# A mixture-of-experts kernel on one core: the routing's arithmetic, the filler matmuls and the order of routing, conversion and weight splits around the first expert are rewritten

## The chip, the cores and the metric

The kernel runs on one core of one Trainium2 chip. The metric is device time in microseconds (us), the median of three runs. The five engines are named as in the profile: PE (TensorE; its weight loads are PEld), DVE (VectorE), ACT (ScalarE), POOL (GpSimd) and SP (SyncE, which here only issues DMAs). Every engine works through its own instructions in program order; an instruction that has to wait holds up all that stand behind it on that engine.

## The reference, cut to what matters

```python
# 1. retention attention: B=4, H=8, S=768, D=64 -> x of 3072 x 512
state = gamma * state + k_t v_t^T;  y_t = 0.125 * q_t state
# 2. routing: 3072 tokens, 8 experts, at most cap = 384 tokens each
for idx in argsort(-(x @ w_gate).flatten()):
    tok, e = idx // 8, idx % 8
    if assigned[tok] < 0 and counts[e] < cap:
        assigned[tok] = e; counts[e] += 1
out[assigned == e] = relu(x[assigned == e] @ w1[e]) @ w2[e]
# 3. dense layer on all tokens, d_ff = 2048
h = out @ w_in
return (max(h, 0) + log1p(exp(-abs(h)))) @ w_out
```

## The kernel before

**Stages.** `Attn` computes the attention in 24 blocks of 128 tokens, stores each block of x to memory (`xd`) and keeps the logits on chip. Beside it `Conv` turns `w_in` from 64-bit to 32-bit floats. Then `Route.phase(0)` finds the first expert that fills up, and the list of its 384 tokens; `fetch_x` (L692) gathers their rows from `xd` with three indirect DMAs that POOL issues. `Ffn.emit` (L835) then works through the eight experts: 24 products of the expert layer (`m1`, `m2`), 16 of the dense layer's first half (`f1`) and 16 of its second (`f2`), always for the 384 tokens of one expert. Every matmul operand is split in a high and a low part, so that each product takes three matmuls: ACT copies the high part, DVE subtracts it to get the low one.

**Routing.** A phase takes each open token's best expert and its logit as a 32-bit key, and looks for the highest key at which some expert has 384 takers. It does so in three levels (bits from 21 up, 10 to 20, 0 to 9), each with a coarse and a fine pass. A pass compares all keys with 46 (or 32) thresholds (DVE, `G`, L429), counts by expert (24 matmuls, L436), compares with the places left (`ind`, L487), counts the thresholds that hold (one matmul, L490) and reduces (`ksat`, L493). The fine pass's threshold comes from `ksat` (`thr`, L476); at its end `base` (L498) is formed, and the next level's keys (`lo`, `kf`, `kx`, L463 to L467). After the levels come the expert (`inc` to `es`, L503 to L528), the mask `mem` (L531 to L534), prefix sums over tokens (two matmul steps), the position of each token as one-hot rows (`ohq`, L567), and the list `ix` (L586). Then the bookkeeping for the next phase (L590 to L615). Phase 0 has nothing beside it: its steps follow each other directly, and in between PE gets filler matmuls (`hum`, L892, 128x512, results unused). The later phases are generators: `emit` calls `route()` once or every other time per product, and `route()` runs to the next `yield`. Their matmuls write a tile `rt`.

**Late conversion.** `w_out` is converted during phase 0 and the first expert: 32 halves of 256 columns. A piece is: `size` (ACT `cA` L270, POOL `cA` L271, ACT `cB` L272), then in one step DVE `cB` (L285), in the next DVE `cA` (L287) and the POOL sum (L288, writes `wol`). There are two `cB` buffers. The kernel before calls `size` for the next piece after this piece's sum. Phase 0 takes two steps in each of the four passes of levels 1 and 2; in the first expert one or two steps are taken after each product, before `route()`. `weights` (L859) splits the weights (`split_w`, L654) up to four products ahead; for a piece of `w_out` it first forces the conversion so far (`until`).

**Order.** Everything is issued in the order in which the Python code runs (a manual schedule); no planner moves instructions.

## Time and profile before

| | us |
|---|---|
| median of three runs | 1018.38 |
| lowest and highest run | 1016.86, 1020.95 |
| the profiled execution | 1018.63 |
| its span in the profile | 1016.9 |
| PE busy | 994.5 (98% of the span) |
| DVE busy | 637.5 (63%) |
| ACT busy | 579.9 (57%) |
| POOL busy | 160.2 (16%) |

Attention lasts until about 112 us of the span, phase 0 and the first gather until 148.5, the first expert until about 257, the other seven experts about 108 us each. PE busy includes fillers, so the busy share says little in phase 0; there the chain of work that ended last (each instruction with what released it) is the view to read. A bracket at the end of a timeline row gives the idle time of the engine before it and what ended it.

### The profile page before, as it was taken

The numbers are of one execution on the slowest core, as the hardware profiler recorded it, in microseconds if no ns is written. First come the engines' busy times: TensorE is split into PE (matmuls) and PEld (weight loads), VectorE is DVE, ScalarE is ACT, GpSimd is POOL, SyncE is SP. The second block draws the span as 40 slices with busy tenths as digits, with TensorE's granted clock in tenths as the row PEclk, the third lists the DMA queues.
The fourth block names the chain that finished last, engine by engine and source line by source line (L and its number), as shares of the span: only waits on it lengthen the run. The fifth ranks groups of instructions, "written<-read, shape, count | busy, mean of one in ns | idle before, by whom it ended". The sixth has DMA issues, their size and how long they took to land.

```text
span 1016.9 us, 19118 instructions
## 1 busy us (share of the span) xinstructions
PE 994.5 (98%) x7319; PEld 899.3 (88%) x7319; DVE 637.5 (63%) x1620; ACT 579.9 (57%) x1250; POOL 160.2 (16%) x185
## 2 busy tenths in 40 slices
PE   9999889999999999999999999999999999999997
PEld 8888669887998889998998899899989999999996
DVE  6989678879666656755575566555665644444442
ACT  5999425777446653665456635654366536653663
POOL 1655223556101010100110010001010010000001
PEclk9999789999999999999999999999999999999999
DMA  9998234224412023200410031103210250013000
GB/s 367 414 415 357 95 115 159 87 71 121 119 39 63 2 68 100 61 1 25 143 57 7 22 125 53 32 11 105 63 32 4 80 166 1 1 57 111 1 1 31
DMA packets 40603, 96.05 MB, mean 94 GB/s; under 512 B 5312, under 2 KB 5568, under 8 KB 40512
## 3 DMA queue, kind: packets, MB, share of 16 engines
q1 hardware_dynamic: 36528, 82.16, 23.9%
q0 software_dynamic: 3840, 12.59, 3.7%
q8 instruction: 57, 0.93, 0.4%
q14 instruction: 34, 0.28, 0.1%
q10 hardware_dynamic: 144, 0.09, 0.0%
HBM read 82.23 MB, written 12.58 MB: 93 GB/s over the span
## 4 chain that ended last, share of the span: by engine, by line
PE 75%; issue 12%; POOL 4%; DVE 4%; ACT 3%; DMA 1%; another core or an unknown queue 0%; POOLq 0%; ACTq 0%
PE h L684 11%; PE h L687 11%; PE h L685 10%; PE acc L782 7%; PE acc L783 7%; PE acc L787 7%; PE acc L676 3%; PE acc L678 3%; PE acc L677 3%; PE pA L130 2%; PE pY L158 2%; PE pX L183 2%; PE rt L436 2%; POOL wol L288 1%; POOL cA L271 1%
## 5 line engine op out<-in xcount | busy, mean ns | idle before, releaser
L748 DVE SCALAR_TENSOR_TENSOR gf<-h,sp 128x384 f32<-128x384 f32 x128 | 71.2, 556 | 186.7 <-ACT sp L746 186.7
L684 PE MATMUL h<-x2h,wih 128*128 128x384 f32 x512 | 175.6, 343 | 1.5 <-DVE xl L672 1.5
L685 PE MATMUL h<-x2h,wil 128*128 128x384 f32 x512 | 172.5, 337 | 0.0
L782 PE MATMUL acc<-whi,gh 128*128 128x512 f32 x384 | 153.3, 399 | 0.0
L783 PE MATMUL acc<-wlo,gh 128*128 128x512 f32 x384 | 151.3, 394 | 0.0
L744 ACT ACTIVATE sp<-h 128x384 f32<-128x384 f32 x128 | 62.4, 487 | 135.6 <-PE h L687 125.3
L668 ACT ACTIVATE h1h<-h 128x384 fp32r<-128x384 f32 x64 | 31.4, 491 | 147.2 <-PE h L687 105.1
L687 PE MATMUL h<-x2l,wih 128*128 128x384 f32 x512 | 112.2, 339 | 0.9 <-DVE x2l L672 0.8
L787 PE MATMUL acc<-whi,gl 128*128 128x512 f32 x384 | 111.2, 396 | 0.8 <-DVE gl L762 0.8
L795 POOL DMA_INDIRECT out_dram<-rows,ix x24 | 24.2, 1007 | 500.0 <-ACT rows L793 496.6
L684 PEld LDWEIGHTS h<-x2h,wih 128*128 128x128 f32 x512 | 96.2, 188 | 5.2 <-DVE xl L672 1.8
L685 PEld LDWEIGHTS h<-x2h,wil 128*128 128x128 f32 x512 | 96.2, 188 | 3.4
L687 PEld LDWEIGHTS h<-x2l,wih 128*128 128x128 f32 x512 | 91.3, 188 | 3.1 <-DVE x2l L672 3.1
L662 DVE TENSOR_TENSOR wlo<-wraw,whi 128x512 fp32r<-128x512 f32 x128 | 86.6, 691 | 6.5 <-ACT whi L661 6.4
L662 DVE TENSOR_TENSOR wlo<-wol,whi 128x512 fp32r<-128x512 f32 x128 | 88.9, 698 | 0.9 <-ACT whi L661 0.9
L684 PE MATMUL h<-xh,whi 128*128 128x384 f32 x256 | 88.2, 345 | 0.7 <-ACT xh L671 0.7
L787 PEld LDWEIGHTS acc<-whi,gl 128*128 128x128 f32 x384 | 72.0, 188 | 18.6 <-DVE gl L762 1.4
L676 PE MATMUL acc<-h1h,whi 128*128 128x384 f32 x256 | 88.4, 345 | 0.0
L661 ACT ACTIVATE whi<-wraw 128x512 fp32r<-128x512 f32 x128 | 76.6, 624 | 17.3 <-DMA wraw<-in_moe_w_dram 16.0
L678 PE MATMUL acc<-h1l,whi 128*128 128x384 f32 x256 | 86.1, 336 | 0.0
L685 PE MATMUL h<-xh,wlo 128*128 128x384 f32 x256 | 86.1, 336 | 0.0
L677 PE MATMUL acc<-h1h,wlo 128*128 128x384 f32 x256 | 86.1, 336 | 0.0
(199 smaller groups left out, 1902.7 us busy)
## 6 DMA issues: line engine op xcount, KB each, us to landing
wraw<-in_moe_w_dram SPq DMA_DIRECT2D x128, 256.0 KB, 2.6
qk_t<-in_qk_dram SPq DMA_DIRECT2D x24, 512.0 KB, 8.6
kv_t<-in_kv_dram SPq DMA_DIRECT2D x24, 512.0 KB, 9.0
raw<-in_moe_w_in_dram SPq DMA_DIRECT2D x16, 512.0 KB, 8.7
raw<-in_moe_w_out_dram SPq DMA_DIRECT2D x32, 256.0 KB, 3.0
xd<-xs SPq DMA_DIRECT2D x24, 256.0 KB, 4.9
rows<-xd,ix POOLq DMA_INDIRECT x24
out_dram<-rows,ix POOLq DMA_INDIRECT x24
```

The source lines that it names most:

```text
L661: nc.scalar.activation(hi, raw, AF.Copy)
L662: nc.vector.tensor_tensor(lo, raw, hi.bitcast(FT), op=OP.subtract)
L676: nc.tensor.matmul(ps, wh, ah, start=start, stop=False)
L677: nc.tensor.matmul(ps, wl, ah, start=False, stop=False)
L678: nc.tensor.matmul(ps, wh, al, start=False, stop=stop)
L684: mm(ps, wh(d), ah[:, d], start=d == 0, stop=False)
L685: mm(ps, wl(d), ah[:, d], start=False, stop=False)
L687: mm(ps, wh(d), al[:, d], start=False, stop=d == 3)
L748: nc.vector.scalar_tensor_tensor(g, ps, 0.0, a, op0=OP.max, op1=OP.add)
L782: nc.tensor.matmul(ps, gh[:, s], wh, start=f == 0, stop=False)
L783: nc.tensor.matmul(ps, gh[:, s], wl, start=False, stop=False)
L787: nc.tensor.matmul(ps, gl[:, s], wh, start=False, stop=f == 15)
```

## The change

1. **Routing arithmetic.** `kx` and the thresholds are scaled by 1/256. The coarse thresholds become constants (`coarse`), numbered so that no pass has to build them. A new `prepare` forms the next level's keys without the base (`kp`) beside the pass before, so that after `base` one operation gives `kx`; `kf` follows after the compare. The matmul after a fine pass multiplies by 4096 (`upto[46, 4096]`). The expert `inc` is read from the last pass's counts (`is_equal` with `k`) instead of a further mask, sum and matmul (which only the last phase keeps). The list's position is masked with 127 in integers.
2. **Filler.** `hum` is 128x256 instead of 128x512; 8, 5, 6, 9, 2, 16 and 30 of them where there were 6, 3, 6, 6, 1, 9 and 16; six more behind the bookkeeping's matmul, and six between the row transposes of the first expert. Phase 0 takes four conversion steps, one each in the first level's fine pass, the second's coarse one and both of the third, instead of eight.
3. **First rows.** `weights(3)` (three splits, and the loads they set free) moves behind the whole of phase 0; the third row tile of the first expert is copied in two halves.
4. **Conversion.** `size` of the next piece moves ahead of this piece's sum, into the step before.
5. **First expert.** `route()` comes before the conversion steps; conversion begins one product earlier; pieces of `w_out` are split two products ahead instead of four; the next expert's rows are fetched behind the first `f1` that finds the list made, not at `f1` number 10. Phase 2 does not begin before the second expert's row transposes, and in the other experts routing pauses during the last two `m2`.

The diff, cut to its core:

```diff
@@ Conv.run
             v.scalar_tensor_tensor(B, w1, UPPER, B, op0=OP.bitwise_and, op1=OP.bitwise_or)
+            if p + self.lead < N:
+                ready.append(self.size(p + self.lead))
             yield
             v.tensor_scalar(A, A, 3, 0x3fffffff, op0=OP.logical_shift_left, op1=OP.bitwise_and)
             nc.gpsimd.tensor_tensor(F, A, B, op=OP.add)
-            if p + self.lead < N:
-                ready.append(self.size(p + self.lead))
             yield
@@ Route
+    def prepare(self, s, sh, mask, off):
+
+        v = self.nc.vector
+        v.tensor_scalar(self.lo[:, s], self.ik[:, s], sh, mask, op0=OP.logical_shift_right, op1=OP.bitwise_and)
+        v.tensor_scalar(self.kp[:, s], self.kf[:, s], -1.0, 4096.0, op0=OP.max, op1=OP.mult)
+        v.scalar_tensor_tensor(self.kp[:, s], self.lo[:, s], off, self.kp[:, s], op0=OP.add, op1=OP.add)
+
@@ Route.phase
             if l:
-                lo = T([128, N], I32, "lo")
-                v.tensor_scalar(lo, self.ik, sh, span - 1, op0=OP.logical_shift_right, op1=OP.bitwise_and)
-                v.tensor_scalar(self.kf, self.kf, base, 4096.0, op0=OP.subtract, op1=OP.mult)
-                off = -4096.0 if l == 1 else 0.0
-                v.scalar_tensor_tensor(self.kf, lo, off, self.kf, op0=OP.add, op1=OP.add)
-                v.tensor_scalar(self.kx, self.bc(self.kf, N, 2), -1.0, 5000.0, op0=OP.max, op1=OP.min)
+                v.tensor_scalar(self.kx, self.bc(self.kp, N, 2), base, S, op0=OP.subtract, op1=OP.mult)
...
-                    fill(l)
+                    if l and not fine:
+                        v.tensor_scalar(self.kf, self.kp, base, 3000.0 if l == 1 else 1.0, op0=OP.subtract,
+                                        op1=OP.min if l == 1 else OP.add)
+                    if l == 1 and fine:
+                        self.prepare(all, 0, 1023, 4096.0)
+                    if i and not l and not fine:
+                        self.prepare(all, 10, 2047, 0.0)
+                    fill(2 * l + fine)
...
-                hum(6 if st == 1 else 3)
+                hum(9 if l == 2 and fine else 6 if fine else 5)
...
+        else:
+            v.tensor_tensor(inc, ps[:, 64:64 + E], k.to_broadcast([128, E]), op=OP.is_equal)
...
-        hum(1)
+        hum(2)
...
-        hum(9)
+        hum(16)
...
-        hum(16)
+        hum(30)
...
+        hum(6)
@@ Ffn.xt
+        if i == 0 and g == T3 - 1:
+            for d in (slice(0, 2), slice(2, 4)):
+                nc.scalar.activation(self.xh[:, d, s], ps[:, d], AF.Copy)
+            nc.vector.tensor_tensor(self.xl[:, :, s], ps, self.xh[:, :, s].bitcast(FT), op=OP.subtract)
+            return
@@ Ffn.emit
         for g in range(T3):
+            if g:
+                self.hum(ps, 6)
             self.xt(0, g)
...
                 while self.listed <= i + 1:
                     self.route()
+                if i + 1 not in self.xg:
+                    self.fetch_x(i + 1)
+            self.weights(at[n] + 4, at[n] + 2)
+            fn(i, f)
+            if fn == self.f1 and f > 1 and self.listed > i + 1 and i + 1 not in self.xg:
                 self.fetch_x(i + 1)
-            self.weights(at[n] + 4)
-            fn(i, f)
-            if i == 0 and n > 3:
+            step += 1
+            hold = self.phase == 1 and self.gen is None if i == 0 else fn == self.m2 and f > 5
+            if not hold and (self.listed <= i + 1 or step % 2 == 0):
+                self.route()
+            if i == 0 and n > 2:
                 for _ in range(1 + n % 2):
                     self.late.step()
-            step += 1
-            if self.listed <= i + 1 or step % 2 == 0:
-                self.route()
...
+    def hum(self, ps, n):
+        a = self.win[0][:, 0]
+        for _ in range(n):
+            self.nc.tensor.matmul(ps[:, 0:256], a[:, 0:128], a[:, 0:256], start=True, stop=True)
@@ Ffn.start
-            for _ in range(2 if level else 0):
+            for _ in range(level in (1, 2, 4, 5)):
                 self.late.step()
...
-            elif mark == "list":
-                self.fetch_x(0)
-                self.weights(3)
+        self.weights(3)
```

DVE in phase 0, from the first level's fine pass to the second level's first compare (before first, then the change; `ind` closes a pass, `cB` is a conversion step):

```order
L476 SCALAR_TENSOR_TENSOR thr<-ksat,jio 128x46
L429 TENSOR_TENSOR G<-kx,thr 128x552
L429 TENSOR_TENSOR G<-kx,thr 128x368
L429 TENSOR_TENSOR G<-kx,thr 128x184
L487 TENSOR_TENSOR ind<-pS,rem 128x8
L493 TENSOR_REDUCE ksat<-pS 128x1
L498 SCALAR_TENSOR_TENSOR base<-ksat 128x1
L463 TENSOR_SCALAR lo<-ik 128x24
L464 TENSOR_SCALAR kf<-kf,base 128x24
L466 SCALAR_TENSOR_TENSOR kf<-lo,kf 128x24
L467 TENSOR_SCALAR kx<-kf 128x48
L474 TENSOR_SCALAR thr<-jio 128x46
```

and in the changed kernel:

```order
L485 SCALAR_TENSOR_TENSOR thr<-ksat,jio 128x46
L435 TENSOR_TENSOR G<-kx,thr 128x552
L435 TENSOR_TENSOR G<-kx,thr 128x368
L435 TENSOR_TENSOR G<-kx,thr 128x184
L285 SCALAR_TENSOR_TENSOR cB<-raw,cB 128x256
L503 TENSOR_TENSOR ind<-pS,rem 128x8
L510 TENSOR_REDUCE ksat<-pS 128x1
L513 SCALAR_TENSOR_TENSOR base<-ksat 128x1
L478 TENSOR_SCALAR kx<-kp,base 128x48
L435 TENSOR_TENSOR G<-kx,coarse_81 128x552
```

Four operations between `base` and the next compare are gone, and a conversion step (`cB`) now stands ahead of `ind`.

DVE in the first expert, at the matmuls of phase 1's third level (`gf`, `gl` belong to the dense layer's first half; `ind` is what PE's `rt` matmul waits for):

```order
L762 TENSOR_TENSOR gl<-gf,gh 128x384
L748 SCALAR_TENSOR_TENSOR gf<-h,sp 128x384
L287 TENSOR_SCALAR cA<-cA 128x256
L285 SCALAR_TENSOR_TENSOR cB<-raw,cB 128x256
L487 TENSOR_TENSOR ind<-rt,rem 128x8
```

and in the changed kernel:

```order
L783 TENSOR_TENSOR gl<-gf,gh 128x384
L769 SCALAR_TENSOR_TENSOR gf<-h,sp 128x384
L503 TENSOR_TENSOR ind<-rt,rem 128x8
L289 TENSOR_SCALAR cA<-cA 128x256
L285 SCALAR_TENSOR_TENSOR cB<-raw,cB 128x256
```

The two conversion operations moved behind `ind`.

## Rows read from the trace of the kernel before

**Rows 1.** Busy PE, PEld, DVE, ACT, POOL by stretch; granted clock, DMA share, GB/s.

```profile
112.10:148.50 36.40, 31.04 (x256) 22.11 (x255) 26.77 (x116) 8.34 (x18) 10.39 (x12) 0.77 0.38 119
187.00:250.00 63.00, 58.52 (x362) 51.24 (x362) 52.88 (x144) 45.81 (x105) 38.55 (x41) 1.00 0.33 98
250.00:1005.00 755.00, 753.65 (x4730) 691.70 (x4729) 433.84 (x1083) 410.88 (x799) 42.26 (x62) 1.00 0.17 52
```

**Rows 2.** Chain that ended last, phase 0 to first product: start, us, what.

```profile
117.25 2.77 PE pA L894 x6
...
143.05 4.09 DMA rows<-xd,ix
...
148.53 0.44 PE h L684
```

**Rows 3.** Timeline of DVE in phase 0: start, us, engine, line, operation.

```profile
116.87 0.17 DVE L487 TENSOR_TENSOR ind<-pS,rem 128x8 bf16<-128x8 f32 x1 [0.47 <-PE pS L436]
...
117.49 0.16 DVE L498 SCALAR_TENSOR_TENSOR base<-ksat 128x1 f32<-128x1 f32 x1
...
118.59 0.87 DVE L429 TENSOR_TENSOR G<-kx,thr 128x552 bf16<-128x552 f16 x3
119.38 0.41 DVE L285 SCALAR_TENSOR_TENSOR cB<-raw,cB 128x256 int32<-128x256 int32 x1
...
120.70 0.17 DVE L487 TENSOR_TENSOR ind<-pS,rem 128x8 bf16<-128x8 f32 x1 [0.71 <-PE pS L436]
...
123.26 0.17 DVE L487 TENSOR_TENSOR ind<-pS,rem 128x8 bf16<-128x8 f32 x1 [0.28 <-PE pS L436]
...
124.20 0.43 DVE L464 TENSOR_SCALAR kf<-kf,base 128x24 f32<-128x24 f32 x1
...
127.08 0.17 DVE L487 TENSOR_TENSOR ind<-pS,rem 128x8 bf16<-128x8 f32 x1 [0.65 <-PE pS L436]
...
129.14 0.17 DVE L487 TENSOR_TENSOR ind<-pS,rem 128x8 bf16<-128x8 f32 x1
...
131.94 0.17 DVE L520 TENSOR_TENSOR inc<-pS,rem 128x8 f32<-128x8 f32 x1 [0.45 <-PE pS L517]
...
139.57 0.16 DVE L586 SCALAR_TENSOR_TENSOR ix<-pS,ix 128x3 int32<-128x3 f32 x1
```

**Rows 4.** Timeline of PE in phase 0: the matmul on `mem`, the fillers after the list.

```profile
133.95 0.18 PE L537 MATMUL pS<-ones,mem 128*128 128x1 bf16 x1
...
139.20 5.49 PE L894 MATMUL pA<-wih 128*128 128x512 f32 x16
```

**Rows 5.** One microsecond of phase 0, columns as in rows 1.

```profile
119.00:120.00 1.00, 1.00 (x8) 0.48 (x7) 1.00 (x5) 0.00 (x0) 0.00 (x0) 0.50 0.00 0
```

**Rows 6.** Timeline of ACT: the first late piece's second copy.

```profile
116.92 0.42 ACT L272 ACTIVATE cB<-raw 128x256 int32<-128x256 uint32 x1
```

**Rows 7.** Timeline of POOL in phase 0: a conversion operation beside the routing.

```profile
123.75 0.84 POOL L271 TENSOR_SCALAR cA<-cA 128x256 f32<-128x256 f32 x1
```

**Rows 8.** Timeline of POOL: last issue of a later gather, beside no other transfer.

```profile
327.00 0.95 POOL L697 DMA_INDIRECT rows<-xd,ix  x1 [0.30 <-issue]
```

**Rows 9.** The stretch behind that gather's landing, columns as in rows 1.

```profile
330.50:331.50 1.00, 1.00 (x6) 0.81 (x5) 1.00 (x3) 0.97 (x3) 0.00 (x0) 1.00 0.00 0
```

**Rows 10.** Who waited for whom, 148 to 256 us: total, times, longest.

```profile
ACT cB L272 <- POOL wol L288: 10.9, 10, 3.0
...
DVE cA L287 <- POOL cA L271: 7.4, 8, 1.4
...
PE h L684 <- DVE xl L672: 1.5, 1, 1.5
PE rt L490 <- DVE ind L487: 1.4, 1, 1.4
...
PE acc L787 <- DVE gl L762: 0.8, 1, 0.8
PE rt L543 <- DVE tb L540: 0.8, 1, 0.8
```

More of the change, by code (lines that the diff above doesn't have):

```diff
@@ L442, in first_part @@
         yield
-        self.compare(c0, c1, self.t0, 46)
+        self.compare(c0, c1, self.coarse[46], 46)
         yield
         self.nc.vector.tensor_scalar(self.kf[:, c0:c1], self.sg[:, c0:c1], 1025.0, None, op0=OP.add)
+        yield
+        self.prepare(slice(c0, c1), 10, 2047, 0.0)
     def phase(self, i, slow=True, hum=lambda n: None, fill=lambda l: None):
@@ L489, in phase @@
                     yield
-                nc.tensor.matmul(ps[:, 64:64 + E], self.upto[J], ind, start=True, stop=True)
-                hum(6 if st == 1 else 3)
+                f = 4096.0 if fine and l < 2 else 1.0
+                nc.tensor.matmul(ps[:, 64:64 + E], self.upto[J, f], ind, start=True, stop=True)
+                hum(9 if l == 2 and fine else 6 if fine else 5)
                 k = T([128, 1], FT, "ksat", bufs=2)
                 v.tensor_reduce(k, ps[:, 64:64 + E], axis=AX.X, op=OP.max)
-                if top is None:
-                    top = k
-                else:
+                if fine:
@@ L497, in phase @@
                     base = T([128, 1], FT, "base")
-                    v.scalar_tensor_tensor(base, top, float(s1), k, op0=OP.mult, op1=OP.add)
-        if base is None:
+                    v.scalar_tensor_tensor(base, top, J * f, k, op0=OP.mult, op1=OP.add)
+                top = k
+        inc = T([128, E], FT, "inc")
+        if last:
             base = 0.0
-        g2 = T([128, 2, N], BF, "g2")
-        gx = T([128, N, 2], BF, "gx")
-        v.tensor_scalar(gx, self.bc(self.kf, N, 2), base, None, op0=OP.is_ge)
@@ L512, in phase @@
-        v.tensor_scalar(g2[:, 1], self.kf, base, None, op0=OP.is_gt)
-        for _ in gap(2):
-            yield
-        if ps is None:
-            ps = self.psum_tile()
-        nc.tensor.matmul(ps[:, 128:128 + E], self.ones, rs[:, 0], start=True, stop=True)
-        hum(6)
-        inc = T([128, E], FT, "inc")
-        v.tensor_tensor(inc, ps[:, 128:128 + E], self.r, op=OP.is_ge)
+            gx = T([128, N, 2], BF, "gx")
+            v.tensor_scalar(gx, self.bc(self.kf, N, 2), base, None, op0=OP.is_ge)
@@ new lines, in phase @@
+            gg = T([128, N, E], BF, "gg")
+            v.tensor_tensor(gg.rearrange("p n (a m) -> p n a m", m=2),
+                            self.oe.rearrange("p n (a m) -> p n a m", m=2),
+                            gx[:, :, None, :].to_broadcast([128, N, E // 2, 2]), op=OP.mult)
+            rs = T([128, E], BF, "rs")
+            with nc.allow_low_precision("counts up to 24"):
+                v.tensor_reduce(rs, gg.rearrange("p c e -> p e c"), axis=AX.X, op=OP.add)
+            for _ in gap(2):
+                yield
@@ L521, in phase @@
+            ps = self.psum_tile()
+            nc.tensor.matmul(ps[:, 64:64 + E], self.ones, rs, start=True, stop=True)
+            v.tensor_tensor(inc, ps[:, 64:64 + E], self.r, op=OP.is_ge)
+        else:
+            v.tensor_tensor(inc, ps[:, 64:64 + E], k.to_broadcast([128, E]), op=OP.is_equal)
+        g2 = T([128, 2, N], BF, "g2")
+        v.tensor_scalar(g2[:, 0], self.kf, base, None, op0=OP.is_ge)
         pr = T([128, E], FT, "pr")
         v.tensor_tensor(pr, inc, self.desc, op=OP.mult)
+        v.tensor_scalar(g2[:, 1], self.kf, base, None, op0=OP.is_gt)
@@ L611, in phase @@
             yield
-        nc.tensor.matmul(ps[:, 136:136 + E], self.ones, rs[:, 1], start=True, stop=True)
+        nc.tensor.matmul(ps[:, 136:136 + E], self.ones, rn, start=True, stop=True)
+        hum(6)
         d2 = T([128, E], FT, "d2")
@@ L841, in emit @@
             n += g[3] is not None
+        ps = self.rps.tile([128, 512], FT, name="rt")
         for g in range(T3):
+            if g:
+                self.hum(ps, 6)
             self.xt(0, g)
@@ L885, in route @@
         self.gen = None
+    def hum(self, ps, n):
+        a = self.win[0][:, 0]
+        for _ in range(n):
+            self.nc.tensor.matmul(ps[:, 0:256], a[:, 0:128], a[:, 0:256], start=True, stop=True)
     def start(self, ps):
-        a = self.win[0][:, 0]
-        def hum(n):
-            for _ in range(n):
-                self.nc.tensor.matmul(ps, a[:, 0:128], a[:, 0:512], start=True, stop=True)
+        hum = lambda n: self.hum(ps, n)
         self.keys = [g[3] for g in self.plan(self.R.E) if g[3]]
```

89 lines of the change are left out of this document (45 added, 44 removed).

## The prediction

> **What bounds the kernel now.** I read the busy time by stretch first. From 250 to 1005 us PE is busy in 753.65 of 755 us [rows 1]: there nothing is to be had, and the change takes no matmul out of it. Two stretches are left. Phase 0 with the first gather, 112.1 to 148.5, takes 36.4 us in which PE does no product of the experts. In 187 to 250 PE stands still for 63.00 - 58.52 = 4.48 us, and by the waits that is four single waits, on `xl` 1.5, `ind` 1.4, `gl` 0.8 and `tb` 0.8, all DVE's [rows 1, 10]. So the change can win at most 4.5 us in the first expert, and in phase 0 what it takes from a chain. That chain is the view to read there: it runs through DVE operations and, which the busy share hides, through the fillers, as the 2.77 us of six fillers at 117.25 [rows 2]. The reader is to see that a filler that is still running when the compare is ready holds up the count behind it on PE.
>
> **Phase 0, part by part.** Times are from the start of `ind` in one pass to the start of `ind` in the next [rows 3].
>
> *A conversion step ahead of the first count.* The first fill now stands in the first level's fine pass, so DVE meets `cB` before the `ind` that ran at 116.87. That `cB` needs ACT's copy of the first piece of `w_out`, which ended at 116.92 + 0.42 = 117.34 since the load had just landed [rows 6]; with its own 0.41 [rows 3], `ind` comes at 117.75. Queued behind the waiting `cB` are `ind`, `ksat` and everything of the next pass. Loss 0.9.
>
> *Coarse passes of levels 2 and 3.* They took 120.70 - 116.87 = 3.83 and 127.08 - 123.26 = 3.82. From `base` to the compare there were six links in 118.59 - 117.49 = 1.10, some 0.2 each; two are left, 0.4. The clock is granted at 0.50 (the level of 1.2 GHz) at 119 [rows 5], and a filler of 512 columns takes 2.77 / 6 = 0.46, so one of 256 columns 0.23 at that level. In the changed pass the six fillers end 0.4 + 1.4 = 1.8 us after `ind`, the first half of the compare 0.6 + 0.4 + 0.5 = 1.5 after it; the 24 counts need about 0.75 (in the fine pass that ended at 129.14 they fit into 2.06 with everything else). Sum 2.5 to 2.6 in place of 3.8: gain 1.3 each, 2.6 together.
>
> *Fine passes.* 123.26 - 120.70 = 2.56 and 129.14 - 127.08 = 2.06. Five half fillers end 0.4 + 1.15 = 1.55 after `ind`, plus 0.75: 2.3 each. Gain 0.26, loss 0.24: nothing.
>
> *From the last pass to the mask.* From `ind` 129.14 to `inc` 131.94 are 2.80 us: `ksat`, `base`, a mask, a product, a sum and a matmul behind fillers. Now `inc` follows `base` (0.62 after `ind`, as 116.87 to 117.49) at 0.8, with one more small operation on the path: gain 1.8. The matmul on `mem` then began at 133.95 [rows 4], seven links of 0.2 behind `inc` being 133.4: the fillers held it 0.5. Nine half fillers at the low level (2.1) end before the mask does: gain 0.5. Together 2.3.
>
> *To the list.* From 133.95 to `ix` at 139.57 are 5.62. One operation goes from the positions, two move behind the first `ohq`, two are swapped for two: gain 0.3. The sixteen half fillers, 3.7 us at the low level, end as the last `ohq` arrives.
>
> Together -0.9 + 2.6 + 0 + 2.3 + 0.3 = 4.3 us at `ix`. The three new operations of `prepare` behind the last compare add under 0.1 here; in the attention they lie beside its matmuls (nine of 0.2 us, 1.8 if that cover failed). The `kp` operations that move into the passes lie beside the counts.
>
> *The rule on the shared port.* A DVE operation of the routing that meets a POOL operation of the conversion is stretched: `kf` at 124.20 took 0.43 beside `cA` at 123.75, where a link is 0.2 [rows 3, 7]. The Trainium skill, SBUF — State Buffer, "Who interferes with whom", speaks against putting `size` one step earlier: DVE in a two-port mode and GpSimd exclude each other, and the later one blocks for the whole instruction. By it each meeting could cost the 0.84 of that POOL operation; the row shows 0.2. There are now two to four such meetings in phase 0 as before, so the sum stays.
>
> **Gather and first product.** From `ix` to the first product are 148.53 - 139.57 = 8.96. The last gather was issued at 143.05 and took 4.09 to land [rows 2] beside three weight loads, which `weights(3)` now sets free only after the gather. Alone, a last issue at 327.00 had landed by 330.50 [rows 8, 9], 3.5: gain 0.6, and 0.3 from copying the last tile in two halves. Against it stand 30 + 6 + 6 + 6 fillers on PE ahead of the last transposes. Sixteen whole ones took 5.49 [rows 4] at a mixed clock; thirty half ones are fifteen whole: 5.2. With three times six half ones at the full clock (half of 0.23 each, 0.7 per six), three sets of transposes of 0.45, and 0.7 to the product, that is 0.2 before `ix` + 5.2 + 2.1 + 1.4 + 0.7 = 9.2. So PE and not the gather would be last: I take +0.2 of gain, with bounds of +0.9 (full clock throughout, gather last) and -2 (most fillers at the low level). Phase 0 gives 4.3 + 0.2 = 4.5, bounds 2.3 and 5.6. DVE's three `wlo`, moved behind the bookkeeping (3 us), end about 6 us after `ix`, before the products want them.
>
> **The first expert.** DVE's lateness behind the four waits has causes that the change takes on. It waited 7.4 us in eight places for POOL's `cA` [rows 10], since that stood behind the piece before's sum in POOL's queue; now it stands ahead. `ind` loses the two conversion operations in front of it (0.5 of its 1.4), and four links of the pass. The rows are fetched one `f1` earlier, off the time of the transposes whose `xl` cost 1.5. A phase loses about 1.7 us of DVE work, two splits move later; two pieces come in from phase 0 (1.4 us). I take 2.5 of 4.5, bounds 0 and 4.4.
>
> What is added is a wait on ACT. With two `cB` buffers, the copy for a piece needs the sum two pieces back, and it is now asked one step after that sum instead of two. Queued behind it are `gh`, `sp` and the weight copies, for which PE waits. ACT waited 10.9 us there in ten places already, 3.0 at most [rows 10].
>
> **Sum.** 4.5 + 2.5 = 7.0. The profiled execution took 1018.63, the median is 1018.38: 1018.38 - 7.0 = 1011.4.
>
> **Rivals.**
> - *The first expert gives nothing:* the ACT wait takes the place of DVE's. For it: 10.9 us already; against it: `gh` is wanted two products after it is made. 1018.4 - 4.5 = 1013.9.
> - *Fillers at the low clock:* thirty run before the chip grants the full clock, transposes come late. For it: 0.77 mean clock in the stretch [rows 1]. Gain 2.3 + 2.5: 1013.6.
> - *The chain is not shortened:* the first `cB` waits longer than the row says, since the load lands when it lands, and counts at the low clock fill what the links give back. Each coarse pass then gives 0.7 instead of 1.3 and the loss is 2: phase 0 gives 2.2, the first expert 0 to 1: 1015.7.
> - *Slower:* ACT becomes the bound of 187 to 250. It is busy 45.81 of 63 [rows 1], 17.2 free. Thirty pieces over some 100 us are 19 here; at the mean wait of today, 1.1, one for each piece costs 21, and from 0.9 per piece on PE waits. To end slower it must eat 4.5 more, from 1.15 per piece; at 1.5, 28.5 - 17.2 - 4.5 = 6.8 lost: 1025.
>
> **How the numbers follow.** Chances: forecast 0.50 (1008.3 to 1013.2), first expert nothing 0.18, low clock 0.13, chain not shortened 0.13, slower 0.06. The range of 1008.0 to 1016.0 takes the first four and the bounds 5.6 + 4.4 and 2.3 + 0. A measurement here can tell 0.5% from no change, which is 5.1 us, 1013.3. Faster: nearly all of the forecast (0.48) and four tenths of the next two (0.12), 0.60; slower 0.05; same 0.35.
>
> **What would show it.** `ind` of the first fine pass about 0.9 us late with `cB` ahead of it; coarse passes of 2.5; `ix` near 135.2; the first product near 144; idle PE in the first expert under 2.5 us, and DVE's wait for POOL's `cA` nearly gone. ACT's wait for the sum well above 10.9 us would show the rival, and transposes that follow a filler without a gap, at a granted clock of 0.50, the other. Wrong would be a shift anywhere behind 250 us.

## The result, and the profile after

The changed kernel takes 1030.62 us (median of five runs, 1029.97 to 1031.05), the kernel before 1019.28 beside it (1016.86 to 1020.95). The ratio is 1.0112, with a 95% interval of 1.0095 to 1.0129: it is **slower by about 11 us**, where 7 us of gain were forecast and 1008 to 1016 was the range. The profiled execution has a span of 1029.3 us against 1016.9.

The first thing to do is to cut the span at marks that both kernels have: the first mask product of the attention, the last row of `L` (the attention's end), and the first product of the experts. Of the kernel before, from DVE's timeline (start, us, engine, line, operation, and in brackets what it waited for):

```profile
7.09 1.29 DVE L134 TENSOR_TENSOR at<-pA,ctab 128x512 f32<-128x512 f32 x2 [3.46 <-PE pA L130]
...
112.13 0.19 DVE L186 TENSOR_REDUCE L<-pX 128x8 f32<-128x32 f32 x1 [1.26 <-PE pX L183]
```

and of the changed kernel, with the marks of phase 0 that answer to [rows 3], and from PE's timeline the first product:

```profile
6.57 1.29 DVE L134 TENSOR_TENSOR at<-pA,ctab 128x512 f32<-128x512 f32 x2 [2.74 <-PE pA L130]
...
114.59 0.19 DVE L186 TENSOR_REDUCE L<-pX 128x8 f32<-128x32 f32 x1 [1.26 <-PE pX L183]
...
120.06 0.16 DVE L503 TENSOR_TENSOR ind<-pS,rem 128x8 bf16<-128x8 f32 x1
122.61 0.17 DVE L503 TENSOR_TENSOR ind<-pS,rem 128x8 bf16<-128x8 f32 x1 [0.21 <-PE pS L442]
125.06 0.17 DVE L503 TENSOR_TENSOR ind<-pS,rem 128x8 bf16<-128x8 f32 x1
127.62 0.17 DVE L503 TENSOR_TENSOR ind<-pS,rem 128x8 bf16<-128x8 f32 x1 [0.29 <-PE pS L442]
129.96 0.17 DVE L503 TENSOR_TENSOR ind<-pS,rem 128x8 bf16<-128x8 f32 x1 [0.59 <-PE pS L442]
130.66 0.16 DVE L533 TENSOR_TENSOR inc<-pS,ksat 128x8 f32<-128x8 f32 x1
...
137.87 0.16 DVE L600 SCALAR_TENSOR_TENSOR ix<-pS,ix 128x3 int32<-128x3 f32 x1
...
146.11 0.45 PE L700 MATMUL h<-xh,whi 128*128 128x384 f32 x1 [0.47 <-ACT xh L728]
```

With the first product of before at 148.53 [rows 2] this gives three stretches:

| stretch | before | after | difference |
|---|---|---|---|
| attention: first mask product to last row of `L` | 105.04 | 108.02 | +2.98 |
| phase 0: last row of `L` to first product | 36.40 | 31.52 | -4.88 |
| first product to the end of the span | 868.37 | 883.19 | +14.82 |

(The other 0.52 are the start: the first mask product came 0.52 us sooner.) Phase 0 did what was forecast. The loss lies in the other two, above all behind the first product. By stretch, with the columns of [rows 1]:

```profile
187.00:250.00 63.00, 55.00 (x324) 47.68 (x323) 44.41 (x120) 38.14 (x89) 31.34 (x36) 0.95 0.27 80
250.00:1005.00 755.00, 749.42 (x4695) 689.47 (x4694) 431.01 (x1067) 413.00 (x804) 47.73 (x69) 1.00 0.18 54
```

In 187 to 250 PE is idle for 8.00 us where it was idle for 4.48, but DVE and ACT work less as well: DVE 44.41 in place of 52.88, ACT 38.14 in place of 45.81. No engine has become the bound; all of them wait, and for each other. Behind 250 the lateness goes on for a while: 5.58 us idle in place of 1.35. For whom they wait, 148 to 256 us, answering to [rows 10] (total, times, longest; `whi` and `wlo` are the high and the low part of a piece of weights):

```profile
POOL wol L290 <- DVE cA L289: 35.2, 17, 4.4
ACT cB L272 <- POOL wol L290: 33.0, 19, 3.9
...
DVE wlo L678 <- ACT whi L677: 16.5, 15, 1.6
...
PE rt L507 <- DVE ind L503: 2.9, 3, 1.7
...
PE rt L559 <- DVE tb L556: 2.9, 1, 2.9
...
PE h L700 <- DVE xl L688: 2.2, 1, 2.2
...
PE acc L804 <- DVE wlo L678: 1.5, 1, 1.5
```

ACT's wait for POOL's sum went from 10.9 us to 33.0, and DVE's wait for ACT, `wlo` for `whi`, from 1.1 us to 16.5. The row of the kernel before is

```profile
DVE wlo L662 <- ACT whi L661: 1.1, 2, 0.7
```

DVE's wait for POOL's `cA` (7.4) is gone, as the prediction said, and what came in its place is dearer. One turn of it, from the timelines of DVE, ACT, POOL and PE:

```profile
213.36 0.45 DVE L285 SCALAR_TENSOR_TENSOR cB<-raw,cB 128x256 int32<-128x256 int32 x1
213.78 0.16 DVE L564 COPY tot<-rt 128x1 f32<-128x1 f32 x1
...
216.04 0.31 DVE L587 TENSOR_TENSOR rh<-dd,cidb 128x144 bf16<-128x144 f32 x1
216.27 0.29 DVE L289 TENSOR_SCALAR cA<-cA 128x256 int32<-128x256 int32 x1
...
216.64 0.85 POOL L290 TENSOR_TENSOR wol<-cA,cB 128x256 int32<-128x256 int32 x1 [2.66 <-DVE cA L289]
...
217.52 0.43 ACT L272 ACTIVATE cB<-raw 128x256 int32<-128x256 uint32 x1 [3.90 <-POOL wol L290]
217.86 0.62 ACT L677 ACTIVATE whi<-wol 128x512 fp32r<-128x512 f32 x1
...
218.51 0.69 DVE L678 TENSOR_TENSOR wlo<-wol,whi 128x512 fp32r<-128x512 f32 x1 [1.62 <-ACT whi L677]
```

Read it from the bottom. DVE waits 1.62 us for `whi`. ACT could not make it because its queue stood for 3.90 us at the copy into `cB`, which needs the buffer that POOL's sum of two pieces back still reads. POOL's sum waited 2.66 us for DVE's `cA`, and that one stood on DVE behind the routing's turn: twelve operations of the routing from `tot` at 213.78 to `rh` at 216.04. So **DVE waits for itself, around POOL and ACT**, and every turn of the routing that it does ahead of a conversion step lengthens the next wait.

### The profile page after: what moved, and what is told of

The parts are those of the page before. It is cut to its first block, busy times and chain, and to the rows that moved or that the text cites. A ratio compares the mean times of both kernels' runs of the same rounds, so it can differ in the third digit from the quotient of the medians.

```text
span 1029.3 us, 19202 instructions
## 1 busy us (share of the span) xinstructions
PE 998.0 (97%) x7357; PEld 908.4 (88%) x7357; DVE 631.1 (61%) x1598; ACT 579.8 (56%) x1251; POOL 157.1 (15%) x185
## 4 chain that ended last, share of the span: by engine, by line
PE 69%; issue 14%; DVE 6%; ACT 4%; POOL 4%; DMA 2%; another core or an unknown queue 0%; SPq 0%; POOLq 0%; ACTq 0%
PE h L700 11%; PE h L703 10%; PE h L701 10%; PE acc L803 7%; PE acc L804 7%; PE acc L808 7%; PE acc L692 3%; PE acc L693 3%; PE acc L694 3%; POOL cA L271 2%; PE rt L442 2%; POOL wol L290 2%; ACT vh L120 1%; PE pA L130 1%; PE pY L158 1%
## 5 line engine op out<-in xcount | busy, mean ns | idle before, releaser
L678 DVE TENSOR_TENSOR wlo<-wol,whi 128x512 fp32r<-128x512 f32 x128 | 89.8, 707 | 13.6 <-ACT whi L677 13.6
```

The source lines that it names most:

```text
L678: nc.vector.tensor_tensor(lo, raw, hi.bitcast(FT), op=OP.subtract)
```

## The experiments

Each run stands beside runs of the kernel before on the same chip. In the table "attention", "phase 0" and "behind" are the three stretches above, from the profiled execution of each. The kernel before had a median of 1017.65 to 1019.32 us from one chip to the next, so runs of different chips are compared by their ratios (e1 to e4 share a chip, e5 to e8, e9 to e12, e13 to e15, and e16 with e17). The stretches come from one execution each. Five executions of the kernel before on one chip lay 4.1 us apart, and kernels with the same attention differ there: 105.06 to 105.82 in seven of them with the sizing late (e1, e5, e6, e9, e10, e11, e13), 107.67 to 109.00 in seven with it early (after, e3, e4, e14 to e17). So a difference of one or two microseconds between two stretches is not shown by these columns alone.

| run | what differs | median us | ratio (95%) | attention | phase 0 | behind |
|---|---|---|---|---|---|---|
| before | | 1017.65 to 1019.32 | 1 | 105.04 | 36.40 | 868.37 |
| after | | 1030.62 | 1.0112 (1.0095 to 1.0129) | 108.02 | 31.52 | 883.19 |
| e1 | after, sizing back, both conversions | 1016.08 | 0.9979 (0.9970 to 0.9989) | 105.82 | 31.54 | 869.62 |
| e2 | before, sizing early | 1028.52 | 1.0106 (1.0089 to 1.0123) | 107.60 | 36.16 | 875.63 |
| e3 | after, third `cB` buffer | 1014.30 | 0.9959 (0.9948 to 0.9970) | 108.62 | 31.43 | 866.31 |
| e4 | after, sizing back in the second conversion | 1018.51 | 1.0002 (0.9992 to 1.0013) | 108.24 | 31.69 | 871.21 |
| e5 | e3 and sizing back in the attention | 1011.88 | 0.9948 (0.9935 to 0.9962) | 105.73 | 31.45 | 866.44 |
| e6 | e5, first conversion step a pass later | 1012.10 | 0.9941 (0.9927 to 0.9955) | 105.32 | 30.60 | 867.47 |
| e7 | e5, prepare out of the attention | 1013.15 | 0.9949 (0.9936 to 0.9963) | 106.02 | 31.52 | 867.18 |
| e8 | before, third buffer, sizing early in the second conversion | 1015.36 | 0.9971 (0.9958 to 0.9983) | 105.59 | 36.30 | 864.54 |
| e9 | e5, split four products ahead | 1013.25 | 0.9947 (0.9929 to 0.9965) | 105.78 | 31.45 | 866.38 |
| e10 | e5, routing's turn behind | 1013.76 | 0.9947 (0.9928 to 0.9967) | 105.77 | 31.20 | 868.17 |
| e11 | e5, both | 1014.52 | 0.9956 (0.9937 to 0.9975) | 105.40 | 31.80 | 868.56 |
| e12 | e3, attention's max behind the sum | 1013.97 | 0.9956 (0.9944 to 0.9969) | 106.64 | 32.11 | 866.70 |
| e13 | e5, eight steps in phase 0 | 1011.76 | 0.9943 (0.9926 to 0.9960) | 105.06 | 32.05 | 865.68 |
| e14 | after, eight steps in phase 0 | 1028.55 | 1.0111 (1.0091 to 1.0131) | 108.71 | 31.69 | 880.21 |
| e15 | after, split four ahead and turn behind | 1023.56 | 1.0061 (1.0045 to 1.0078) | 108.27 | 31.31 | 874.40 |
| e16 | after, split four ahead | 1030.41 | 1.0110 (1.0092 to 1.0128) | 107.67 | 31.72 | 882.03 |
| e17 | after, routing's turn behind | 1022.87 | 1.0033 (1.0021 to 1.0044) | 109.00 | 31.67 | 875.26 |

**The theory** after the two traces: ACT's copy for the next piece waits for the sum of two pieces back, and what DVE and PE need stands behind it (A). **The rival:** the new order of routing and splits makes the waits by itself (B). A third, for the attention: prepare's operations (C).

### Four runs that tell the sizing from the order

*e1*, the one edit undone:

```
             v.scalar_tensor_tensor(B, w1, UPPER, B, op0=OP.bitwise_and, op1=OP.bitwise_or)
-            if p + self.lead < N:
-                ready.append(self.size(p + self.lead))
             yield
             v.tensor_scalar(A, A, 3, 0x3fffffff, op0=OP.logical_shift_left, op1=OP.bitwise_and)
             nc.gpsimd.tensor_tensor(F, A, B, op=OP.add)
+            if p + self.lead < N:
+                ready.append(self.size(p + self.lead))
             yield
```

> The kernel after, with the sizing of the next piece moved back behind this piece's sum, in both conversions; all other edits stay. Theory A (ACT waits for the sum of two pieces back, and what PE needs stands behind it): the last row of L lands near 112.1 again instead of 114.6, idle PE in the first expert (187 to 260 us) falls from 12.3 to about 4, ACT's wait for the sum from 35.9 us to about 11; time 1013 to 1016. Rival B (the routing's turn ahead of the conversion, or w_out split one piece ahead, makes the waits): only the 2.4 us of the attention come back, 1027 to 1029. Rival C (prepare's operations make the attention late): the row of L stays at 114.6.

1016.08, just over the upper edge of A's range and far from B's. Of the 14.8 us behind the first product 13.6 are gone, and the attention is back at 105.82. In 148 to 256 us the waits read

```profile
ACT cB L272 <- POOL wol L288: 16.9, 11, 3.5
DVE cA L287 <- POOL cA L271: 8.2, 8, 1.4
```

so ACT's wait is half of 33.0, though not back at 10.9, and DVE's wait for POOL's `cA` has returned.

*e2*, the same lines moved the other way in the kernel before, and nothing else:

> The kernel before with this one edit alone: the sizing of the next piece ahead of this piece's sum. Theory A: slower by the attention's 2.4 us and by most of the first expert's 12 to 15, so 1030 to 1035; ACT's wait for the sum rises from 10.9 us to over 25. Rival B: 2 to 3 us slower at most, 1021 to 1022, and ACT's wait stays under 15.

1028.52: the one edit alone loses about 10 us, 2.56 in the attention and 7.3 behind the first product. ACT's wait, 148 to 256 us:

```profile
ACT cB L272 <- POOL wol L290: 24.5, 17, 2.8
```

The direction is A's, though the time and the wait both stay a little under what A asked for (1030 and 25); the size is about half of what the same edit costs in the kernel after (7.3 against 13.6). That difference is taken up below.

*e3*, which takes away what ACT waits for and moves no instruction:

```
-    F.late, F.kept = Conv(tc, ctx, 256, halves, 3), kept
+    F.late, F.kept = Conv(tc, ctx, 256, halves, 3, 1, (3, 3)), kept
...
-        nx = T([128, N, E], BF, "nx")
+        nx = T([128, N, E], BF, "gg")
```

(three more small routing tiles share a buffer in the same way, to make room for 1 KB per partition)

> The kernel after with a third cB buffer in the second conversion (the room comes from four small routing tiles that share a buffer with another tile); the order of instructions on every engine stays that of the kernel after. Theory A: the copy asks for the sum of three pieces back, ACT's wait for it falls from 35.9 us to under 8, idle PE in the first expert goes back to about 4; the attention keeps its 2.4: 1015 to 1019. Rival B: the order is unchanged, so is the time: 1029 to 1031.

1014.30, a little better than A asked for; B is out, since the order is that of the kernel after. In 148 to 256 us:

```profile
ACT cA L270 <- DMA raw<-in_moe_w_out_dram: 10.7, 8, 3.1
...
DVE wlo L678 <- ACT whi L677: 4.2, 6, 1.1
...
PE h L700 <- DVE xl L688: 2.0, 2, 1.0
```

ACT's copy into `cB` no longer waits for the sum; of such waits one of 0.6 us is left, at its copy into `cA`. It runs ahead until it waits for the load of the next piece, and PE's waits are short again. The stretch of 187 to 250 shows all engines at work again:

```profile
187.00:250.00 63.00, 59.02 (x384) 51.59 (x383) 55.90 (x148) 48.38 (x111) 38.26 (x42) 1.00 0.33 101
```

*e4*, the sizing back in the second conversion only:

```
-            if p + self.lead < N:
+            if self.lead > 1 and p + self.lead < N:
                 ready.append(self.size(p + self.lead))
             yield
...
+            if self.lead == 1 and p + self.lead < N:
+                ready.append(self.size(p + self.lead))
```

> The kernel after with the sizing moved back behind the sum in the second conversion only; the attention's conversion keeps it ahead. Against the run with it back in both, this prices the attention's share: theory A 1015.5 to 1018.5, 2.4 us over that run. If the attention's lateness has another cause (prepare), the two are equal. Rival B: 1029 to 1031.

1018.51, at the upper edge of A's range, and 2.43 over e1 on the same chip: the attention's share comes from its own conversion, whose two pieces of lead and four `cB` buffers are another case.

### The two losses apart, and what was forecast right

*e5* puts the third buffer and the attention's old order together (the lines of e4 with the two conditions exchanged, and those of e3).

> The kernel after with the third cB buffer in the second conversion, where the sizing stays ahead of the sum, and with the sizing back behind the sum in the attention's conversion. Theory A (the two losses are separate: a cB buffer of two pieces back in the first expert, and the attention's own 2.4 us): the run with the third buffer alone had 1014.3, less 2.4 is 1011.9, range 1011 to 1013. Rival (the third buffer only moved the wait, and the earlier end of the attention is given back in the first expert): 1014 or more.

1011.88, as the sum of the two said: the attention is back at 105.73, and behind the first product it stays at e3's length. (The ratios of e3 and e5 overlap in their intervals, so by the time alone the two are not apart.) This version is faster than the kernel before by 0.5% (0.38 to 0.65%) and than the kernel after by 1.6% (0.9948 / 1.0112).

*e6*:

```
-            for _ in range(level in (1, 2, 4, 5)):
+            for _ in range(level > 1):
```

> As the run before it, and the first conversion step of phase 0 moved from the fine pass of the first level to the coarse pass of the second (fills in passes 2, 3, 4 and 5 in place of 1, 2, 4 and 5, so as many steps). Theory A: the first count no longer stands behind a copy that waits for a load; the pass that took 2.47 us from ind to ind falls by about 0.9: 1011.0. Rival: the same wait meets the next pass, nothing gained: 1011.9.

Phase 0 gets shorter by 0.85 us, as said: `ind` of the first fine pass comes 4.75 us behind the last row of `L` in place of 5.44. Behind the first product the profiled execution has 1.03 more, and the time is the same (1012.10 and 1011.88). The profile shows the cost of the early step in phase 0, and the time does not show it.

*e7*, prepare taken out of `first_part` and done once behind the compare of phase 0's first fine pass:

```
-        yield
-        self.prepare(slice(c0, c1), 10, 2047, 0.0)
...
-                    if i and not l and not fine:
+                    if not l and fine == (i == 0):
```

> As the first run of this call, but prepare for the first phase is not done in the attention: its three operations come once, for all rows, behind the compare of phase 0's first fine pass. If prepare is covered in the attention, as the prediction says, this costs the three operations there at most, 0 to 0.6 us: 1012 to 1012.5. If the nine operations delay the attention (the row of L came 0.8 us later against the attention's first row than before, with the sizing back), it is 0.2 to 0.8 faster.

1013.15, no gain: the attention keeps its length (106.02 and 105.73), so the nine operations were covered there as far as the spread of this stretch (0.8 us) can tell, and C falls.

*e8*, third buffer and early sizing in the second conversion of the kernel before:

> The kernel before with two edits: a third cB buffer in the second conversion (two routing tiles share a buffer to make room) and the sizing ahead of the sum there. Theory A: with room for it the earlier sizing takes DVE's 7.4 us wait for POOL's cA away and costs ACT nothing: 1016 to 1018. Rival (the order of POOL's queue, a max ahead of the sum that waits for ACT, costs by itself): 1020 or more.

1015.36, a little under A's range, and 3.8 us less behind the first product. So where the edit in this conversion cost 7.3 us by itself (e2), the edit and one more buffer, 1 KB per partition, together gain 2.5 to 3. What the buffer would gain without the early sizing no run shows, since none gives the kernel before the third buffer alone. The order of POOL's queue, which the early sizing changes as well, shows no cost here.

### Why the same wait costs twice as much in the kernel after

Behind the first product e8 has 864.5 us and e5 866.4, and early sizing with two buffers costs 7.3 in one kernel and 13.6 in the other. Of what differs there are three suspects: the split two products ahead, the routing's turn ahead of the conversion, and the steps that phase 0 no longer does. First with the third buffer in.

*e9*: `self.weights(at[n] + 4)` again.

> The version with the third cB buffer in the second conversion and the attention's sizing back (1011.88 us), and with it w_out split four products ahead again in the first expert instead of two. From the first product to the end that version took 866.4 us, the kernel before with the same two edits 864.5. If the late split costs the 1.9: 1010. If it only moves DVE's work: 1011.5 to 1012.5. If DVE's splits that come sooner hold up xl and gl: 1013.

*e10*: the routing's turn behind the conversion steps again.

```
+            if i == 0 and n > 2:
+                for _ in range(1 + n % 2):
+                    self.late.step()
             step += 1
             hold = self.phase == 1 and self.gen is None if i == 0 else fn == self.m2 and f > 5
             if not hold and (self.listed <= i + 1 or step % 2 == 0):
                 self.route()
-            if i == 0 and n > 2:
-                for _ in range(1 + n % 2):
-                    self.late.step()
```

> The same version with the routing's turn behind the conversion steps again. If the turn ahead of the conversion is what the forecast took it for (ind without two conversion operations in front of it, 0.5 us): 1012 to 1013. If it costs the 1.9 us behind the first product: 1010.

*e11*: both.

> The same version with both undone, the split two pieces ahead and the routing's turn behind. If the 1.9 us come from these two orders together: 1010. If they come from the two pieces that phase 0 no longer converts: 1012 or more.

The ratios of the three are 0.9947, 0.9947 and 0.9956, that of e5 0.9948: with room in the buffers neither order can be told from the other by the time. By the profile the routing's turn ahead is worth 1.7 us behind the first product (866.44 against 868.17), but the profiled execution of e10 was the slowest of its four (1014.38, the fastest 1012.64), so this gain is not shown.

*e12* asks what it is in the attention:

```
             if p + self.lead < N:
-                ready.append(self.size(p + self.lead))
+                ready.append(self.size(p + self.lead, self.lead == 1))
             yield
             v.tensor_scalar(A, A, 3, 0x3fffffff, op0=OP.logical_shift_left, op1=OP.bitwise_and)
             nc.gpsimd.tensor_tensor(F, A, B, op=OP.add)
+            if self.lead > 1 and p + self.lead < N:
+                self.floor(ready[-1][0])
```

(`floor` is POOL's max, taken out of `size`)

> The kernel after with the third cB buffer in the second conversion, the attention's sizing early on ACT as in the kernel after, but POOL's max of the next piece behind this piece's sum as before. If the attention's 2.4 us come from POOL's queue (a max that waits for ACT stands ahead of the sum that ACT and DVE need): 1011.9, the last row of L about 105.7 us behind the first mask product of the attention. If they come from ACT's own order (two copies of the next piece ahead of the copies that the attention needs): 1014.3, the row 108.4 behind.

The attention takes 106.64 us, where e3 took 108.62 and e5 105.73, and this lies outside of both groups named above: by the profile about two of the 2.9 us come from POOL's queue. In the kernel after, the timelines of DVE and POOL read

```profile
63.09 0.42 DVE L289 TENSOR_SCALAR cA<-cA 128x512 int32<-128x512 int32 x1
...
63.77 1.49 POOL L271 TENSOR_SCALAR cA<-cA 128x512 f32<-128x512 f32 x1 [2.90 <-ACT cA L270]
65.22 1.69 POOL L290 TENSOR_TENSOR cA<-cA,cB 128x512 int32<-128x512 int32 x1
```

and in e12 POOL's reads

```profile
62.59 1.28 POOL L294 TENSOR_TENSOR cA<-cA,cB 128x512 int32<-128x512 int32 x1 [2.40 <-DVE cA L293]
63.83 1.93 POOL L277 TENSOR_SCALAR cA<-cA 128x512 f32<-128x512 f32 x1
```

In the kernel after the sum had its `cA` from DVE at 63.51, but the max stood ahead of it and waited for ACT (2.90 us idle in all), so the sum began 1.7 us later than it could. It ended at 66.91 in place of 63.87, and ACT's copy of it into `wih` began at 66.94 in place of 65.71 (0.32 us of these differences is the later start of that execution). The other 0.9 would be ACT's own order. By the time none of this is shown: the ratio of e12, 0.9956, lies inside the intervals of both e3 and e5, and in its profile phase 0 was 0.7 longer.

*e13* and *e14* put eight conversion steps into phase 0 again, as the kernel before has them, with and without the third buffer:

```
-            for _ in range(level in (1, 2, 4, 5)):
+            for _ in range(2 if level > 1 else 0):
```

> The version with the third cB buffer in the second conversion and the attention's sizing back, with eight conversion steps in phase 0 as in the kernel before (two in each pass of the second and third level) in place of four. The twin with one step in each of these passes had 10.2 less in phase 0 than nothing to compare with: 30.60 us from the row of L to the first product and 867.47 behind it. If the pieces that phase 0 no longer converts cost the first expert 1.9 us: 865.5 behind the first product, and phase 0 longer by 4 steps of about 0.5, 32.5: no change in time, 1012. If they cost nothing there: 1014.

(The clause on 10.2 in it is a slip of the pen; the two figures behind it are those of e6.) 1011.76: 1.8 us less behind the first product than e6, 1.45 more in phase 0, no change in time, as forecast: work that is taken from phase 0 would then be paid for in the first expert.

> The kernel after, two cB buffers and all, with eight conversion steps in phase 0 in place of four. The earlier sizing alone lost 7.2 us behind the first product when added to the kernel before, and 13.6 us when taken out of the kernel after. If the difference comes from the pieces that are left for the first expert: 877 behind the first product in place of 883.2, phase 0 up to 2 us longer, 1026. If it comes from the order of routing and splits: 883, 1031 to 1033.

880.21 behind the first product: by the profile the steps account for 3.0 of the 14.8 at most, less than half of the difference that was asked about. By the time they account for nothing (1.0111 and 1.0112).

*e15* to *e17* undo the orders with two buffers, where ACT does wait:

> The kernel after with the routing's turn behind the conversion again and w_out split four products ahead; sizing early, two cB buffers, four steps in phase 0. If the orders make the wait for the sum so much dearer (a split asks for a piece at the last moment, while ACT stands): 877 behind the first product, 1024. If the pieces do: 883, 1030.6.

> The kernel after with w_out split four products ahead again; the routing's turn stays ahead of the conversion, sizing early, two cB buffers. With both orders undone the loss behind the first product fell from 883.2 to 874.4 us. If the late split makes the wait dear (a split needs its piece at the last moment, and wlo waited 17.4 us for whi): about 875 behind the first product, 1023 to 1025. If the routing's turn does: 883, 1030.

> The kernel after with the routing's turn behind the conversion steps again; the split stays two products ahead, sizing early, two cB buffers. If the routing's turn ahead makes the wait dear (the sum that ACT waits for stands behind the routing's operations on DVE, since POOL's sum needs DVE's cA): about 875 behind the first product, 1023 to 1025. If the late split does: 883, 1030.

e15 has 874.40 behind the first product, e16 882.03 and e17 875.26. So the late split costs 1.2 at most, and **the routing's turn ahead of the conversion makes the wait dear**: 7.9 of the 14.8 us, and about 8 in time (1.0112 and 1.0033). Undoing the split as well is no help: e15, with both undone, has 1.0061. In e17, 148 to 256 us:

```profile
ACT cB L272 <- POOL wol L290: 25.9, 18, 3.0
...
DVE wlo L678 <- ACT whi L677: 8.7, 9, 1.6
```

That is the loop of the timeline above: with the routing first, the sum that ACT waits for has the routing's operations ahead of it on DVE. With three buffers the same turn costs nothing that the time shows (e10); there ACT no longer waits for that sum (e3).

## Why the prediction was wrong, and where it was right

- **Phase 0: right.** Forecast 4.5 (2.3 to 5.6), measured 4.88. A conversion step ahead of the first count: forecast 0.9 lost; `ind` came 5.47 behind the last row of `L` in place of 4.74, so 0.73, and e6 that undoes it shows 0.69. The chain of waits of the kernel after (start, us, what) has the load, ACT's two copies and DVE's `cB` in a row, as the prediction read it:

```profile
115.90 2.94 DMA raw<-in_moe_w_out_dram
118.92 0.44 ACT cA L270
119.36 0.33 ACT cB L272
119.72 0.43 DVE cB L285
...
141.09 3.84 DMA rows<-xd,ix
144.98 0.67 PE h L724 x4
```

- Coarse passes: 2.55 and 2.56 us in place of 3.83 and 3.82, gain 2.54 where 2.6 was said. Fine passes: 2.45 and 2.34, together 0.17 lost, where no change was said. From the last `ind` to `ix` 7.91 in place of 10.43: 2.52, where 2.3 and 0.3 were said.
- From `ix` to the first product 8.24 in place of 8.96, 0.72 where 0.2 was said. The step that failed is that PE would be last: the gather was (3.84 to land, and the transposes 0.05 behind it). The thirty fillers did not take 5.2 us: the next matmul that is no filler began 3.7 us after the first of them, and the granted clock was 1.00 from 137.9 to 141. That is the case for which the prediction gave its upper bound, 0.9.
- **The attention: wrong, 2.98 lost where nothing was counted.** The prediction covered the nine operations of prepare, rightly (e7), and did not cost the sizing there at all. The change moves it in both conversions; its working followed it only in the second. That is 2.4 us by e1 and e4; the rest lies within the spread of this stretch.
- **The first expert: wrong, by 17.3 us.** With ACT's wait taken away (e3) the stretch behind the first product is 2.06 shorter than before, where 2.5 was said, but this does not show the 2.5: a third buffer is in it, and the kernel before with that buffer and the early sizing alone is shorter still (e8, 864.54). With the sizing back and all else kept (e1) it is 869.62, no gain. What failed is the last step of that part, the wait on ACT. It was named with its place, its cause and its queue, and then put at nothing in the sum; where a rival does price it, it is set against the 17.2 us that ACT had free.
- The rival for slower had the wait and its queue, but not how it costs. ACT waited 33.0 us for 27 pieces in 148 to 256, which is 1.22 and beyond the rival's point of decision, 1.15. That it came out slower there is luck: in e17 it is 25.9 us for 29 pieces, 0.89, at which the formula loses nothing, and the stretch behind the first product is still 6.9 us longer than before. By the formula nineteen pieces at 1.22 are 23.2 us, 6.0 beyond the 17.2 that ACT had free, and 1.5 after the further 4.5 that the formula takes off; measured are 14.8 behind the first product and 11.3 in the time. It treated a wait as busy time that fills an engine's spare time. ACT was never full, its busy time even fell to 38.14. In the turn shown above the wait of 3.90 us delayed `whi`, which stood behind it, though ACT had time free, and it came round to DVE, which had been waited for.
- The second failed step is in the same place: the routing's turn ahead of the conversion was booked as a gain of 0.5 on `ind`, and I did not ask who waits for the conversion's `cA` that it pushes back. That order is worth about 8 us of loss with two buffers (e17) and no difference that the time shows with three (e10).
- **The rule on the shared port** was weighed for phase 0 only. There the passes came out as said, with their meetings. In the first expert the early sizing makes new ones: of 30 `cA` operations of DVE in 116 to 262 us, nine overlap a conversion operation of POOL, none does so in the kernel before (all took 0.28 or 0.29), and there are none with the sizing back (e1). Four of the nine took 0.83 or 0.84, as the first of these rows, beside which the second stands:

```profile
209.09 0.83 DVE L289 TENSOR_SCALAR cA<-cA 128x256 int32<-128x256 int32 x1
...
208.92 0.85 POOL L290 TENSOR_TENSOR wol<-cA,cB 128x256 int32<-128x256 int32 x1 [2.95 <-DVE cA L289]
```

- All four end 0.14 or 0.15 us after the POOL operation ends. The Trainium skill, SBUF — State Buffer, "Who interferes with whom", has the later of the two, DVE in a two-port mode and GpSimd, blocked for the whole instruction, and these rows agree. The other five took 0.39 to 0.48. Two of them, which began as the POOL operation neared its end, end 0.14 or 0.15 us after it too. Three, all beside POOL's max `cA`, ended 0.3 us before the POOL operation did, so they were only slowed: there the rows differ from the rule, and the rows count. The nine cost DVE some 3 us (four times 0.55, five times 0.1 to 0.2). e5 has eight such meetings, four of them of 0.82 or 0.83, and is fast, so they aren't the cause of the loss.
- "Wrong would be a shift anywhere behind 250 us": there was one, 4.2 us more of idle PE in 250 to 1005. ACT's last copy of a piece is at 260.56, where the kernel before had it at 246.73.

What stays open: how the 14.8 us divide is known only by single undos (third buffer 16.9, sizing 13.6, turn 7.9, steps 3.0, split 1.2), each from one profiled execution, which overlap and don't add up; what the third buffer gains by itself; and in the attention the share of ACT's own order.

## What to carry to other kernels

Before an instruction that takes a buffer is moved forward, follow the buffer's release through every in-order queue that it passes, and look whether the chain comes back to the engine that will wait; if it does, a wait is not paid from spare time but turns up on all engines at once as less busy time. Look then for one more buffer before looking for another order: here early sizing in the second conversion cost 7.3 us with two buffers and, with 1 KB per partition more, is part of a gain, and the order of routing and conversion, worth 8 us before, no longer shows in the time. And if an edit sits in a function that two places use, its price is worked out in both.

## What the runs showed of the hardware that was not expected

A stall of PE can cost more than it lasts, by the clock behind it. After the wait of 2.88 us for `tb` the granted clock reads (columns as in [rows 1], the clock is the third from the end)

```profile
210.00:213.50 3.50, 0.62 (x4) 0.28 (x3) 2.36 (x5) 3.44 (x9) 1.69 (x3) 0.98 0.24 75
213.50:216.50 3.00, 3.00 (x11) 3.00 (x11) 2.79 (x15) 0.12 (x1) 0.48 (x1) 0.50 0.32 87
217.00:220.00 3.00, 3.00 (x17) 2.60 (x16) 1.16 (x2) 2.42 (x6) 1.30 (x2) 1.00 0.32 87
```

0.50 is the level of 1.2 GHz. PE's timeline shows the products of 384 columns 0.32 us apart there:

```profile
214.35 0.52 PE L700 MATMUL h<-x2h,wih 128*128 128x384 f32 x1
214.67 0.52 PE L701 MATMUL h<-x2h,wil 128*128 128x384 f32 x1
```

where they are 0.17 apart at the full clock (146.57, 146.74, 146.91 behind the first product). Twelve products from 213.56 to the next ones at 217.19 took 3.63 us; at 0.17 each they take 2.0, so the stall of 2.88 cost another 1.6. Two more stretches of the kernel after have a mean far below 1.00:

```profile
236.00:241.00 5.00, 3.55 (x10) 2.47 (x10) 3.93 (x11) 2.73 (x8) 3.51 (x4) 0.66 0.25 70
260.00:265.00 5.00, 5.00 (x41) 4.42 (x40) 4.90 (x15) 4.35 (x10) 1.73 (x2) 0.66 0.02 3
```

In the first the clock fell after waits of 0.76 and 1.45 us with one matmul of 0.50 between them, in the second 1.4 us after a wait of 2.10, with PE at work in between. Not every stall did this: behind 1.72 us at 200 to 202 and 2.16 at 250.5 to 252.7 the next two to three us read 1.00. In 187 to 250 the mean is 0.95, in the kernel before 1.00 [rows 1], though PE waited four times there too. So part of the loss behind the first product is no idle time at all: from there to the end PE's busy time rises from 855.40 us to 861.94 and its idle time from 12.97 to 21.25, which is 8.3 of the 14.8 us. The three stretches lack 0.50 of the clock for 3 us and 0.34 for 5 us twice, so an estimate from these rows gives them about 5 of the other 6.5.
